# Eight small expert layers: four experts at a time as column tiles, a later k scale, and a first weight loaded early

## The chip, the cores and the metric

One core of one Trainium2 chip runs the kernel. The metric is the device time in microseconds of one execution, as a median of runs. A profile's span is about 1.8 us shorter than the time of the run it was taken from. In the profiles PE is the matrix engine and PEld its weight loads; DVE, ACT and POOL are the vector, scalar and GpSimd engines. A transfer (DMA) is issued by an engine and lands later, which is when its data may be used. The lead is the stretch before the loop is in full swing.

## The reference, cut to what matters

```python
# attention over (8 batches, 12 heads, 448 tokens, 64)
q_n, k_n = rmsnorm(q, g_q), rmsnorm(k, g_k)
attn = softmax(q_n @ k_n.T / 8) ; x = (attn @ v) as (3584, 768)
# soft mixture of experts: 8 experts with 4 slots each
logits = x @ phi                           # (3584, 32)
d = softmax over tokens ; slot_input = d.T @ x     # (32, 768)
for e in range(8):
    h = np.maximum(slot_input[e] @ w1[e], 0)       # (4, 768) @ (768, 1024)
    slot_out[e] = h @ w2[e]                        # (4, 1024) @ (1024, 768)
out = softmax over slots of logits @ slot_out      # (3584, 768)
```

The work is 24 quads of four heads each, then 16 weight matrices of 3 MB in f32 for only 32 rows, then an output of 11 MB.

## The kernel before

The loop runs over quads; one load of q brings two of them (an octet of heads). In quad Q the scores and the exponentials of Q are made, and between them the preparation of later quads: squares, row sums, `rsqrt` (Ln and Exp on ACT), scaling on POOL, transposes on PE.

```python
for Q in range(NQ + 2):
    ...                                    # score(Q, 0), square, norm, trans(Q+2, 0) ... cut
    if Q + 1 < NQ:
        trans(Q + 1, 1); evac(Q + 1, 1)    # k of the next quad: PE, then a DVE copy
    ... rowsum(Q + 4, 0)                   # DVE
    score(Q, 3) ; ... ; norm(Q - 1, 1, 1) ; rowsum(Q + 2, 1)
    score(Q, 4) ; moe_x(Q - 1)
    rsqrt(Q + 4, ...) ; scaleqk(Q + 2, 1)  # ACT, then POOL scales k with the new factors
    ...
    for i, wq in enumerate(WQ):            # WQ = [0, 2, 4, 7, 9, 11, 14, 16, 18, 19, 20, ...]
        if wq == Q: loadw(i)               # POOL issues a weight's load, f32 to bf16
```

Nine weights have room of their own. Weights 9 to 14 go where the loop's buffers were; the last goes where weight 0 was. After the loop each expert uses the weights as the stationary side:

```python
def layer1(e):                             # 48 matmuls of 4 columns, each with its 128x128 load
    hp = psum.tile([128, FC, Spe], F32, tag="sc", name="hTp")
    for fc in range(FC):
        for dc in range(DC):
            nc.tensor.matmul(hp[:, fc], wt[2 * e][:, dc, fc * 128:(fc + 1) * 128],
                             sinT[:, dc, e * Spe:(e + 1) * Spe], ...)
    nc.vector.tensor_scalar(hTs[:, e], hp, 0.0, None, op0=mybir.AluOpType.max)
# layer2(e) the same with 48 more; 8 experts, then six transposes and the output stage
```

The softmax here doesn't subtract the row's maximum and nothing guards it: scores larger than these inputs give would overflow.

Of the kernel before, what the change touches and what calls it, by code (L numbers as in the profile page):

```python
# [8 lines left out]
F32 = mybir.dt.float32  # L9
# [9 lines left out]
def kernel(  # L19
# [12 lines left out]
    nc = tc.nc  # L32
# [16 lines left out]
    NPRE = 9  # L49
    C0 = [0, 128, 256, 320]  # L50
# [22 lines left out]
    for i in range(2):  # L73
        place("rawq", 2 * 4 * NT * D, 1)
        place("rawk", 2 * 2 * NT * D, 1)
        place("free", 768, 1)
    place("rawk", 2 * 2 * NT * D, 1)
    place("sq", 2 * 2 * 2 * NT * D, 1)
    place("qkn", 2 * NT * 128, 1)
    place("vraw", 2 * 2 * NT * D, 2)  # L80
# [17 lines left out]

    def wsrc(i):
        e = i // 2  # L100
        if i % 2 == 0:
            return moe_w1[e].rearrange("(dc dp) f -> dp dc f", dp=128)
        return moe_w2[e].rearrange("(fc fp) d -> fp fc d", fp=128)
# [6 lines left out]
    wview = lambda ap, i: ap.rearrange("p (c f) -> p c f", c=DC if i % 2 == 0 else FC)  # L110
# [59 lines left out]
    gg = const.tile([128, 1], F32)  # L170
    phi_s = const.tile([128, DC, NS], BF16)
# [21 lines left out]
    def sq(t):  # L193
        return at("sq", 0).bitcast(F32).rearrange("p (t x) -> p t x", t=2)[:, t]
# [22 lines left out]
    def qkn(Q, t):  # L217
        return at("qkn", Q).rearrange("p (t s c) -> p t s c", t=2, s=NT)[:, t]
# [148 lines left out]
    vcopy(0)  # L367

    WQ = [0, 2, 4, 7, 9, 11, 14, 16, 18, 19, 20, 21, 22, NQ - 1, NQ]
    DONE = {max((b * DC + dc) // 4 * 2 + dc % 2 for dc in range(DC)): b for b in range(B)}  # L370

    for Q in range(NQ + 2):
# [3 lines left out]
        if Q == 0:  # L376
            load4(3, 1)
            loadq(2)
        elif Q + 4 < NQ:
            load4(Q + 4, 1)  # L380
# [3 lines left out]
        if Q == 0:  # L384
            rsqrt(3, 1, 2)
            scaleqk(1, 1, nc.vector)
            rowsum(2, 0)
            square(2, 1)
            rowsum(2, 1)
            trans(1, 0)  # L390
            evac(1, 0)
        else:
            if Q + 4 < NQ:
                square(Q + 4, 0)
            if Q + 2 < NQ:
                square(Q + 2, 1, True)
# [24 lines left out]
        if Q + 1 < NQ:  # L421
            trans(Q + 1, 1)
            evac(Q + 1, 1)
        if Q == 0:
            rsqrt(4, 1, 2)
            scaleqk(2, 1)
            rowsum(3, 0)
        elif Q + 4 < NQ:
            rowsum(Q + 4, 0)
# [22 lines left out]
        if on:  # L452
            score(Q, 4)
        if 0 <= Q - 1 < NQ:
            moe_x(Q - 1)
        if Q == 0:
            loadq(3)
            rowsum(4, 0)
            rsqrt(4, 0, 1)
        elif Q + 2 < NQ:  # L460
            rsqrt(Q + 4, 0 if Q + 4 < NQ else 1)
            scaleqk(Q + 2, 1)
# [9 lines left out]
        if on:  # L472
            score(Q, 6)
            ov(Q, 0, 1)
            norm(Q, 0, 0)
        if Q == 1:
# [8 lines left out]
    sinT = at("xT", 0)[:, DC * NS:2 * DC * NS].rearrange("p (dc s) -> p dc s", dc=DC)  # L485
    nc.vector.tensor_tensor(sinT, sacc[:, :DC], dinv.unsqueeze(1).to_broadcast([128, DC, NS]), op=MUL)

# [14 lines left out]

    hTs = at("xT", 1)[:, :E * FC * Spe].rearrange("p (e fc s) -> p e fc s", e=E, fc=FC)
    soTr = at("xT", 2)[:, :HD]
    so4 = at("xT", 3)[:, :HD]

    def layer1(e):
        hp = psum.tile([128, FC, Spe], F32, tag="sc", name="hTp")
        for fc in range(FC):
            for dc in range(DC):  # L510
                nc.tensor.matmul(hp[:, fc], wt[2 * e][:, dc, fc * 128:(fc + 1) * 128],  # L511
                                 sinT[:, dc, e * Spe:(e + 1) * Spe], start=(fc == 0 and dc == 0),
                                 stop=(dc == DC - 1), skip_group_check=True)
        nc.vector.tensor_scalar(hTs[:, e], hp, 0.0, None, op0=mybir.AluOpType.max)

    def layer2(e):
        sp = psum.tile([128, DC, Spe], F32, tag="misc", name="soTp")

        order = [(fc, dc) for dc in range(DC) for fc in range(FC)]
        for fc, dc in sorted(order) if e == E - 1 else order:  # L520
            nc.tensor.matmul(sp[:, dc], wt[2 * e + 1][:, fc, dc * 128:(dc + 1) * 128],  # L521
                             hTs[:, e, fc], start=(dc == 0 and fc == 0),
                             stop=(fc == FC - 1), skip_group_check=True)
        nc.vector.tensor_copy(soTr.rearrange("p (dc r s) -> p dc r s", dc=DC, r=4)[:, :, :, e * Spe:(e + 1) * Spe],
                              sp.unsqueeze(2).to_broadcast([128, DC, 4, Spe]))

    layer1(0)
    for fc in (0, FC // 2):
        nc.gpsimd.dma_start(out=wt[2 * E - 1][:, fc:fc + FC // 2], in_=wsrc(2 * E - 1)[:, fc:fc + FC // 2])
    for e in range(E):  # L530
        if e + 1 < E:
            layer1(e + 1)
        layer2(e)


    sop = psum.tile([128, HD], BF16, tag="misc", name="sop")
    for dc in range(DC):
        nc.tensor.transpose(sop[:, dc * 128:(dc + 1) * 128], soTr[:, dc * 128:(dc + 1) * 128], ident)
    nc.vector.tensor_copy(so4, sop)
# [51 lines left out]
```

## Time and profile before

| What | us |
|---|---|
| time, median | 285.3 |
| loop ends, first expert matmul | 218.2 |
| last weight has landed | 243.3 |
| output stage starts | 250.4 |
| end of the span | 282.9 |

Read the table from below: the output stage is 32.5 us of writing. It starts 7.1 us after the last weight has landed. The lines of the profile are in the prediction.

### The profile page before, as it was taken

Reading aid. Unit: us, or ns where it says so; the run is one execution under the profiler, and the core shown is the slowest. Engines: PE = TensorE matmul, PEld = TensorE weight load, DVE = VectorE, ACT = ScalarE, POOL = GpSimd, SP = SyncE. Lnnn points to the kernel's source line nnn. Section 1 sums busy time; section 2 is a strip of 40 time slices with the busy share of each in tenths; the row PEclk is TensorE's granted clock in tenths of the full one; section 3 lists DMA queues with packets and bytes.
Section 4 is the critical chain, followed back from the end, with each engine's and each line's share of the span. In section 5 each row is a group of like instructions: output and inputs, shape, how many; then the busy total and the mean of one; then the engine's idle time right before and its main releaser. Section 6 shows DMA issues by size and latency. Waiting matters only on the chain.

```text
span 282.9 us, 8520 instructions
## 1 busy us (share of the span) xinstructions
PE 222.4 (79%) x3588; PEld 148.1 (52%) x3588; DVE 179.8 (64%) x384; ACT 190.8 (67%) x276; POOL 168.4 (60%) x188
## 2 busy tenths in 40 slices
PE   7658888989898889989888998998986765788800
PEld 2325555556565556656555665665565765743300
DVE  3776677778878777787877777876564110148800
ACT  4399699888888998888889988899960000036600
POOL 0479699989688989888699896998311200000000
PEclk9955899999999999999999999999997555555555
DMA  7994999999999999999999998999999999129995
GB/s 209 325 288 132 238 255 297 243 305 231 260 259 216 279 259 260 266 267 278 284 204 238 302 220 208 233 221 230 212 211 213 211 213 210 33 92 374 420 425 248
DMA packets 42087, 69.82 MB, mean 247 GB/s; under 512 B 3776, under 2 KB 30912, under 8 KB 42048
## 3 DMA queue, kind: packets, MB, share of 16 engines
q1 hardware_dynamic: 26336, 44.05, 50.6%
q0 software_dynamic: 15392, 25.22, 49.1%
q8 instruction: 28, 0.46, 0.6%
q14 instruction: 11, 0.09, 0.1%
q10 hardware_dynamic: 320, 0.00, 0.1%
HBM read 83.46 MB, written 11.01 MB: 334 GB/s over the span
## 4 chain that ended last, share of the span: by engine, by line
PE 41%; DVE 22%; ACT 10%; issue 5%; ACTq 0%
DVE ss L210 11%; PE ov L284 10%; PE sc L272 7%; ACT arena L273 6%; PE qkTp L239 6%; PE hTp L511 4%; PE op L551 4%; PE soTp L521 4%; DVE arena L244 4%; DVE arena L294 3%; PE sinp L332 2%; PE op L552 2%; DVE arena L314 2%; ACT ss L214 1%; PE eTp L342 1%
## 5 line engine op out<-in xcount | busy, mean ns | idle before, releaser
L273 ACT ACTIVATE arena<-sc 128x896 bf16<-128x896 f32 x168 | 143.2, 921 | 7.9 <-PE sc L272 5.6
L222 POOL TENSOR_TENSOR arena<-arena,rs 128x896 bf16<-128x896 f32 x47 | 80.5, 1713 | 29.6 <-issue 11.1
L284 PE MATMUL ov<-arena 128*128 128x65 bf16 (+1 forms) x1344 | 64.4, 200 | 0.5 <-DVE arena L294 0.5
L284 PEld LDWEIGHTS <-arena 128*128 128x128 bf16 x1344 | 50.1, 99 | 20.4 <-issue 19.7
L272 PE MATMUL sc<-arena 64*128 64x448 bf16 x288 | 53.5, 368 | 7.8 <-ACT arena L273 7.1
L210 DVE TENSOR_REDUCE ss<-arena 128x14 f32<-128x896 f32 x48 | 51.6, 1076 | 5.9 <-ACT arena L202 5.9
L294 DVE TENSOR_TENSOR arena<-ov,rd 128x256 bf16<-128x256 f32 x96 | 40.7, 424 | 3.3
L555 ACT ACTIVATE wown<-op,arena 128x768 f32<-128x768 f32 x14 | 12.4, 899 | 41.2 <-PE op L552 41.2
L200 POOL TENSOR_TENSOR arena<-arena 128x896 f32<-128x896 f32 x21 | 35.4, 1686 | 0.3
L239 PE MATMUL qkTp<-ident,arena 128*128 128x128 bf16 x336 | 28.3, 227 | 6.0 <-POOL arena L222 5.4
L272 PEld LDWEIGHTS <-arena 64*128 64x128 bf16 x288 | 16.6, 93 | 25.1 <-issue 13.5
L311 PE MATMUL xTp<-ident,arena 128*128 128x128 bf16 x192 | 18.9, 222 | 12.9 <-DVE arena L294 12.9
L202 ACT ACTIVATE arena<-arena 128x896 f32<-128x896 f32 x27 | 25.6, 951 | 3.4 <-DMA arena<-in_q_dram 2.5
L239 PEld LDWEIGHTS <-arena 128*128 128x128 bf16 x336 | 20.3, 101 | 12.6 <-POOL arena L222 7.0
L293 DVE RECIPROCAL rd<-ov 128x4 f32<-128x4 f32 x96 | 17.0, 177 | 11.8 <-PE ov L284 11.4
L244 DVE COPY arena<-qkTp 128x896 bf16<-128x896 bf16 x24 | 15.0, 623 | 14.5 <-PE qkTp L239 14.5
L255 DVE TENSOR_SCALAR arena<-qkTp,gg 128x896 bf16<-128x896 bf16 (+1 forms) x26 | 17.5, 680 | 7.6 <-PE qkTp L239 7.6
L311 PEld LDWEIGHTS <-arena 128*128 128x128 bf16 x192 | 10.8, 97 | 21.6 <-DVE arena L294 17.0
L214 ACT ACTIVATE ss<-ss,eps 128x28 f32<-128x28 f32 (+1 forms) x29 | 9.1, 313 | 18.1 <-DVE ss L210 18.1
L314 DVE COPY arena<-xTp 128x1024 bf16<-128x1024 bf16 x24 | 16.4, 683 | 2.6 <-PE xTp L311 2.6
L557 DVE TENSOR_SCALAR wown<-op,arena 128x768 f32<-128x768 f32 x14 | 14.2, 1017 | 4.6 <-PE op L552 4.4
L551 PE MATMUL op<-arena,eT 32*128 32x512 bf16 x28 | 16.0, 616 | 1.4 <-ACT wown L555 0.7
(62 smaller groups left out, 215.4 us busy)
## 6 DMA issues: line engine op xcount, KB each, us to landing
wown<-in_moe_w_dram POOLq DMA_DIRECT2D x9, 1536.0 KB, 16.0
arena<-in_k_dram SPq DMA_DIRECT2D x24, 448.0 KB, 7.7
arena<-in_q_dram SPq DMA_DIRECT2D x11, 896.0 KB, 8.5
arena<-in_moe_w_dram POOLq DMA_DIRECT2D x6, 1536.0 KB, 16.8
out_dram<-wown SPq DMA_DIRECT2D x11, 768.0 KB, 8.3
arena<-in_v_dram SPq DMA_DIRECT2D x48, 128.0 KB, 6.8
arena<-in_v_dram SPq DMA_DIRECT2D x48, 96.0 KB, 6.7
out_dram<-wown SPq DMA_DIRECT2D x6, 384.0 KB, 7.0
```

The lines of the kernel that those rows point to most:

```text
L200: nc.gpsimd.tensor_tensor(s, r, r, op=MUL)
L202: nc.scalar.activation(out=s, in_=r, func=ACTF.Square)
L210: nc.vector.reduce_sum(sss[n][:, t], sq(t).rearrange("p (r d) -> p r d", d=D), axis=AX)
L222: (eng or nc.gpsimd).tensor_tensor(qkn(Q, t).rearrange("p s (r d) -> p s r d", r=2), raw(Q, t).rearrange("p r (s d) -> p s r d", d=D), rs. ...
L239: nc.tensor.transpose(pts[t][:, i], qkn(Q, t)[:, s], ident)
L244: nc.vector.tensor_copy(kT(Q).rearrange("p w (s c) -> p w s c", s=NT), pt.rearrange("p s (w c) -> p w s c", w=2))
L272: nc.tensor.matmul(sc[:, j, :S], kT(Q)[r, i // 4, c0:c0 + 128], qT(Q)[r, i // 4], start=True, stop=True)
L273: nc.scalar.activation(out=attn(i), in_=sc[:, :, :S], func=ACTF.Exp, scale=0.125)
L284: nc.tensor.matmul(ovs[half][:, c, o0:o0 + m], attn(i)[:, j, c0:c0 + 128], mov, start=(n == 0 and c == 0), stop=(n == 6), skip_group_check ...
L294: nc.vector.tensor_tensor(xq(Q).rearrange("p c (h w d) -> p c h w d", h=2, w=2)[:, 2 * half:2 * half + 2, :, w], o[:, :, :, :D], rd.to_bro ...
L311: nc.tensor.transpose(xps[Q][:, i], xq(Q)[:, i % 4, i // 4 * 128:i // 4 * 128 + 128], ident)
L551: nc.tensor.matmul(op[:, 0], eTtok(j, s), so4[r, :512], start=True, stop=True, tile_position=tp)
```

## The change

Its intent has three parts. **Experts**: the weights become the moving side, 512 columns long; the 32 slots of the input are the stationary side, and four experts sit side by side in the four 32-column strips of the array. Each strip computes all 32 slots for its expert, a mask (`own`) keeps the four that are its own, and a 0/1 matrix (`sel`) adds the strips up at the end. **Loop**: k is scaled at the start of the next quad, from factors that exist by then, and its transpose and copy stand behind the row sums. The load of a later k moves behind that scaling, and the loop's buffers are regrouped (lines cut here). **Early weights**: weight 0 is issued in the lead, weights 1 to 8 one quad earlier.

```diff
+    WORD = [(l, EG * g + j) for g in range(E // EG) for l in range(2) for j in range(EG)]
...                                                     (experts)
+        if Q == 2:
+            for j in range(EG):
+                r = slice(NS * j, NS * j + NS)
+                nc.vector.tensor_copy(sel[r]..., ident[r, r]...to_broadcast([NS, EG, NS]))
+                for g in range(E // EG):
+                    nc.vector.reduce_sum(own[r, g:g + 1], ident[r, o:o + Spe], axis=AX)
...
+    def layer1(g):
+        hp = psum.tile([128, 2, 512], F32, tag="sc", name="hp")
+        for dc in range(DC):
+            for i in range(2):
+                for j in range(EG):
+                    nc.tensor.matmul(hp[NS * j:NS * j + NS, i], sinT[:, dc],
+                                     wt[2 * EG * g + j][:, dc, i * 512:i * 512 + 512], ...,
+                                     tile_position=(0, NS * j))
...
+    layer2(0, range(EG))
+    layer2(1, (0, 1))
+    layer2(1, (2,))
+    layer2(1, (3,), range(FC // 2))
+    layer2(1, (3,), range(FC // 2, FC))
...                                                     (loop)
-            scaleqk(Q + 2, 1)                           # end of quad Q
+            if Q + 1 < NQ:
+                scaleqk(Q + 1, 1)                       # start of quad Q
+        if Q and Q + 1 < NQ:                            # now behind score(Q, 4)
+            trans(Q + 1, 1)
+            evac(Q + 1, 1)
...                                                     (early weights)
-    WQ = [0, 2, 4, 7, 9, 11, 14, 16, 18, 19, 20, 21, 22, NQ - 1, NQ]
+    loadw(0)
+    WQ = [-1, 1, 3, 6, 8, 10, 13, 15, 17, 19, 20, 21, 22, NQ - 1, NQ]
```

More of the change, by code (lines that the diff above doesn't have):

```diff
@@ L49 @@
     NPRE = 9
+    EG = 4
     C0 = [0, 128, 256, 320]
@@ L71, in place @@
             sizes.append(elems)
-    for i in range(2):
-        place("rawq", 2 * 4 * NT * D, 1)
-        place("rawk", 2 * 2 * NT * D, 1)
-        place("free", 768, 1)
+    place("rawq", 2 * 4 * NT * D, 1)
+    place("sq0", 2 * 2 * NT * D, 1)
+    place("free", 768, 1)
+    place("rawq", 2 * 4 * NT * D, 1)
     place("rawk", 2 * 2 * NT * D, 1)
-    place("sq", 2 * 2 * 2 * NT * D, 1)
-    place("qkn", 2 * NT * 128, 1)
-    place("vraw", 2 * 2 * NT * D, 2)
+    place("free", 768, 1)
+    place("rawk", 2 * 2 * NT * D, 1)
+    place("sq1", 2 * 2 * NT * D, 1)
+    place("qkn0", NT * 128, 1)
+    place("vraw", 2 * 2 * NT * D, 1)
+    place("rawk", 2 * 2 * NT * D, 1)
+    place("qkn1", NT * 128, 1)
+    place("vraw", 2 * 2 * NT * D, 1)
     place("kT", 2 * S, 1)
@@ L96, in at @@
         return arena[:, off:off + elems]
+    WORD = [(l, EG * g + j) for g in range(E // EG) for l in range(2) for j in range(EG)]
     def wsrc(i):
-        e = i // 2
-        if i % 2 == 0:
+        l, e = WORD[i]
+        if l == 0:
             return moe_w1[e].rearrange("(dc dp) f -> dp dc f", dp=128)
@@ L109 @@
     wplace += [arena[:, o:o + WSZ], wplace[0]]
-    wview = lambda ap, i: ap.rearrange("p (c f) -> p c f", c=DC if i % 2 == 0 else FC)
+    wview = lambda ap, i: ap.rearrange("p (c f) -> p c f", c=(DC, FC)[WORD[i][0]])
     wt = [wview(wplace[i], i) for i in range(2 * E)]
@@ L170 @@
     gg = const.tile([128, 1], F32)
+    sel = const.tile([128, 128], BF16)
+    own = const.tile([128, E // EG], F32)
     phi_s = const.tile([128, DC, NS], BF16)
@@ L193, in sq @@
     def sq(t):
-        return at("sq", 0).bitcast(F32).rearrange("p (t x) -> p t x", t=2)[:, t]
+        return at(f"sq{t}", 0).bitcast(F32)
     def square(Q, t, pool=False):
@@ L217, in qkn @@
     def qkn(Q, t):
-        return at("qkn", Q).rearrange("p (t s c) -> p t s c", t=2, s=NT)[:, t]
+        return at(f"qkn{t}", 0).rearrange("p (s c) -> p s c", s=NT)
     def scaleqk(Q, t, eng=None):
@@ L378 @@
             loadq(2)
-        elif Q + 4 < NQ:
-            load4(Q + 4, 1)
         if on:
@@ L394 @@
                 square(Q + 4, 0)
+            if Q + 1 < NQ:
+                scaleqk(Q + 1, 1)
+            if Q + 4 < NQ:
+                load4(Q + 4, 1)
             if Q + 2 < NQ:
@@ L420 @@
             norm(Q - 1, 1, 0)
-        if Q + 1 < NQ:
-            trans(Q + 1, 1)
-            evac(Q + 1, 1)
         if Q == 0:
-            rsqrt(4, 1, 2)
-            scaleqk(2, 1)
+            trans(1, 1)
+            evac(1, 1)
             rowsum(3, 0)
@@ L458 @@
             rowsum(4, 0)
-            rsqrt(4, 0, 1)
+            rsqrt(4)
         elif Q + 2 < NQ:
             rsqrt(Q + 4, 0 if Q + 4 < NQ else 1)
-            scaleqk(Q + 2, 1)
         if on:
@@ L475 @@
             norm(Q, 0, 0)
+        if Q == 2:
+            for j in range(EG):
+                r = slice(NS * j, NS * j + NS)
+                nc.vector.tensor_copy(sel[r].rearrange("p (r s) -> p r s", r=EG),
+                                      ident[r, r].unsqueeze(1).to_broadcast([NS, EG, NS]))
+                for g in range(E // EG):
+                    o = NS * j + (EG * g + j) * Spe
+                    nc.vector.reduce_sum(own[r, g:g + 1], ident[r, o:o + Spe], axis=AX)
         if Q == 1:
@@ L484, with turn, layer2 @@
     nc.vector.reciprocal(dinv, sacc[:, DC])
-    sinT = at("xT", 0)[:, DC * NS:2 * DC * NS].rearrange("p (dc s) -> p dc s", dc=DC)
+    sinT = at("xT", 0)[:, :DC * NS].rearrange("p (dc s) -> p dc s", dc=DC)
     nc.vector.tensor_tensor(sinT, sacc[:, :DC], dinv.unsqueeze(1).to_broadcast([128, DC, NS]), op=MUL)
+    hTs = {}
+    def layer1(g):
[3 more added lines that the diff above has]
+                for j in range(EG):
+                    nc.tensor.matmul(hp[NS * j:NS * j + NS, i], sinT[:, dc], wt[2 * EG * g + j][:, dc, i * 512:i * 512 + 512],
+                                     start=(dc == 0), stop=(dc == DC - 1), skip_group_check=True, tile_position=(0, NS * j))
+        h = at("x", 2 * g)
+        for i in range(2):
+            nc.vector.tensor_scalar(h[:, i * 512:i * 512 + 512], hp[:, i], 0.0, own[:, g:g + 1], op0=mybir.AluOpType.max, op1=MUL)
+        return h
+    def turn(g, h):
+        ht = psum.tile([128, FC, 128], BF16, tag="misc", name="ht")
+        for fc in range(FC):
+            nc.tensor.transpose(ht[:, fc], h[:, fc * 128:fc * 128 + 128], ident)
+        hTs[g] = at("x", 2 * g + 1).rearrange("p (fc c) -> p fc c", fc=FC)
+        nc.vector.tensor_copy(hTs[g], ht)
+    def layer2(g, js, fcs=range(FC)):
+        for fc in fcs:
+            for c0, c1 in ((0, 512), (512, HD)):
+                for j in js:
+                    nc.tensor.matmul(sop[NS * j:NS * j + NS, c0 // 512, :c1 - c0], hTs[g][:, fc, NS * j:NS * j + NS],
+                                     wt[2 * EG * g + EG + j][:, fc, c0:c1], start=(g == 0 and fc == 0),
+                                     stop=(g == 1 and fc == FC - 1), skip_group_check=True, tile_position=(0, NS * j))
+    h = layer1(0)
+    for fc in (0, FC // 2):
+        nc.gpsimd.dma_start(out=wt[2 * E - 1][:, fc:fc + FC // 2], in_=wsrc(2 * E - 1)[:, fc:fc + FC // 2])
+    turn(0, h)
+    h = layer1(1)
     def eTtok(j, s):
@@ L501 @@
         nc.vector.reciprocal(cinv[:, j:j + 2], cs[:, :, :SO])
-    hTs = at("xT", 1)[:, :E * FC * Spe].rearrange("p (e fc s) -> p e fc s", e=E, fc=FC)
-    soTr = at("xT", 2)[:, :HD]
-    so4 = at("xT", 3)[:, :HD]
-    def layer1(e):
-        hp = psum.tile([128, FC, Spe], F32, tag="sc", name="hTp")
-        for fc in range(FC):
-            for dc in range(DC):
-                nc.tensor.matmul(hp[:, fc], wt[2 * e][:, dc, fc * 128:(fc + 1) * 128],
-                                 sinT[:, dc, e * Spe:(e + 1) * Spe], start=(fc == 0 and dc == 0),
-                                 stop=(dc == DC - 1), skip_group_check=True)
-        nc.vector.tensor_scalar(hTs[:, e], hp, 0.0, None, op0=mybir.AluOpType.max)
@@ L516, in layer2 @@
-    def layer2(e):
-        sp = psum.tile([128, DC, Spe], F32, tag="misc", name="soTp")
-        order = [(fc, dc) for dc in range(DC) for fc in range(FC)]
-        for fc, dc in sorted(order) if e == E - 1 else order:
-            nc.tensor.matmul(sp[:, dc], wt[2 * e + 1][:, fc, dc * 128:(dc + 1) * 128],
-                             hTs[:, e, fc], start=(dc == 0 and fc == 0),
-                             stop=(fc == FC - 1), skip_group_check=True)
-        nc.vector.tensor_copy(soTr.rearrange("p (dc r s) -> p dc r s", dc=DC, r=4)[:, :, :, e * Spe:(e + 1) * Spe],
-                              sp.unsqueeze(2).to_broadcast([128, DC, 4, Spe]))
@@ L527 @@
-    layer1(0)
-    for fc in (0, FC // 2):
-        nc.gpsimd.dma_start(out=wt[2 * E - 1][:, fc:fc + FC // 2], in_=wsrc(2 * E - 1)[:, fc:fc + FC // 2])
-    for e in range(E):
-        if e + 1 < E:
-            layer1(e + 1)
-        layer2(e)
-    sop = psum.tile([128, HD], BF16, tag="misc", name="sop")
-    for dc in range(DC):
-        nc.tensor.transpose(sop[:, dc * 128:(dc + 1) * 128], soTr[:, dc * 128:(dc + 1) * 128], ident)
-    nc.vector.tensor_copy(so4, sop)
+    turn(1, h)
+    sop = psum.tile([128, 2, 512], F32, tag="sc", name="sop")
@@ new lines @@
+    layer2(0, range(EG))
[3 more added lines that the diff above has]
+    layer2(1, (3,), range(FC // 2, FC))
+    so = at("xT", 2)[:, :HD]
+    so4 = at("xT", 3)[:, :HD]
+    parts = ((0, 512, nc.scalar.copy), (512, HD, nc.vector.tensor_copy))
+    for c0, c1, copy in parts:
+        copy(so[:, c0:c1], sop[:, c0 // 512, :c1 - c0])
+    for c0, c1, copy in parts:
+        sp = psum.tile([128, 512], F32, tag="misc", name="sp")
+        nc.tensor.matmul(sp[:, :c1 - c0], sel, so[:, c0:c1], start=True, stop=True)
+        copy(so4[:, c0:c1], sp[:, :c1 - c0])
```

## The prediction

> **What bounds the kernel now.** I read the page first, then the stretches (busy time of each engine by stage), the chain of waits, the timeline of one quad, and the landings of the weight transfers.
>
> The page's slices, and then the same split where the behaviour changes:
>
> ```profile
> PEclk9955899999999999999999999999997555555555
> DMA  7994999999999999999999998999999999129995
> ...
> q1 hardware_dynamic: 26336, 44.05, 50.6%
> q0 software_dynamic: 15392, 25.22, 49.1%
> ```
>
> ```profile
> 20.00:30.00 10.00, 7.52 (x70) 4.64 (x68) 6.56 (x13) 9.30 (x16) 9.40 (x10) 0.50 0.65 148
> 30.00:135.00 105.00, 90.65 (x1432) 60.58 (x1430) 82.63 (x181) 91.20 (x133) 90.12 (x97) 0.99 1.10 263
> 135.00:145.00 10.00, 8.48 (x135) 5.83 (x135) 7.62 (x18) 9.05 (x14) 7.66 (x9) 1.00 0.93 247
> ...
> 170.00:180.00 10.00, 8.46 (x134) 5.50 (x134) 8.34 (x18) 8.70 (x13) 7.68 (x9) 1.00 0.89 223
> 180.00:217.00 37.00, 32.91 (x586) 22.42 (x584) 23.67 (x63) 27.22 (x38) 20.76 (x27) 0.98 1.13 217
> 217.00:243.00 26.00, 16.00 (x574) 15.77 (x575) 3.57 (x16) 0.00 (x0) 1.50 (x2) 0.50 1.08 198
> 243.00:250.00 7.00, 6.38 (x214) 6.13 (x211) 1.38 (x6) 0.00 (x0) 0.00 (x0) 0.50 0.02 5
> 250.00:283.00 33.00, 16.95 (x56) 7.01 (x55) 14.49 (x15) 12.38 (x14) 0.00 (x0) 0.50 0.81 334
> ```
>
> Columns: length, busy us of PE, PEld, DVE, ACT, POOL, then granted clock, DMA share, GB/s. The reader is to see four stages: lead (to 30 us), quad loop (to 217), experts (217 to 250), output (to 283). The DMA share is 1.06 to 1.13 nearly everywhere from 5 to 243 us; packets of two queues overlap, so about 1.1 is what full engines look like here. From 243 to 250 it is 0.02: every weight has landed, and PE alone still works. In the output it is DMA again (11 MB at 420 GB/s is 26 of the 33 us).
>
> The loop looks bound by a chain through engines:
>
> ```profile
> 119.96 0.40 PE qkTp L239 x7
> 120.36 0.02 issue
> 120.38 0.62 DVE arena L244
> 121.01 0.99 DVE ss L210
> 122.00 0.10 DVE rd L293
> 122.10 0.02 issue
> 122.12 0.42 DVE arena L294
> 122.55 1.00 DVE ss L210
> 123.55 0.02 issue
> 123.58 0.33 ACT ss L214
> ```
>
> The transpose of the next k, its eviction on DVE, two row sums behind it, and ACT's Ln, which waits for the second sum. The list of waits for 27 to 217 us gives its price:
>
> ```profile
> ACT ss L214 <- DVE ss L210: 12.5, 19, 1.0
> ```
>
> A quad takes 7.75 us, or 8.88 where the slot weights are worked on (starts of ACT's Square, 118.55 and 126.51 or 109.87).
>
> The experts are neither matmul work nor weight transfers:
>
> ```profile
> 227.79 2.37 issue
> 230.16 0.33 PE hTp L511 x7
> 230.48 1.28 PE soTp L521 x48
> 231.76 1.28 PE hTp L511 x48
> 233.04 0.67 PE soTp L521 x25
> 233.71 2.37 issue
> ```
>
> 7+48+48+25 is 128 matmuls, with their loads 256 instructions, then PE stands 2.4 us. The four gaps (1.82, 2.37, 2.37, 2.60) are 5.9 to 6.1 us apart from end to end, and the trace has an instruction transfer of 16384 bytes beside each: 256 instructions of 64 bytes. I read this as PE running dry of instructions.
>
> Landings of the last weights, from the trace: 196.9, 204.9, 212.9, 220.9, 228.4, 235.9, and the last one's halves at 239.6 and 243.3: one per 7.5 us.
>
> **What the Trainium skill says.** "DMA: Bandwidth & Descriptors", section Queues, rings and completion order: each DMA engine goes round the queues it has work for. So a weight in flight takes from q, k and v. The trace agrees: in 70 to 75 us the weight queue moved 160 GB/s and the other 65, and in 75 to 80, the weight landed, 26 and 309. The same page, section Where 436 GB/s comes from, gives 435 GB/s for the fabric. Weights alone write 209 GB/s of bf16 and so read 418 of f32: the engines are at their rate, and only idle time can be won.
> "TensorE: Matmul & The Clock Gate", section Part 3: Packing small matmuls, measures 2.38 times for three column tiles of 512 columns. The kernel before has no pure column tiles of that length; its 64x64 pairs (four of 448 columns in 0.57 us) do overlap. The same page, section Back-to-back issue gap, gives N/1.2 ns cold and about N/2.4 warm; 24 four-column matmuls tell nothing of that here, but the 512-column ones of the output start 0.43 us before the next, which is 512/1.2 at the granted 0.50.
>
> **The change, part by part.**
>
> 1. Experts. 768 matmuls of 4 columns with 768 loads of 128x128 go, and 8 DVE steps each of ReLU and copy. In come, for each group of four experts, 48 matmuls of 512 columns in rounds of four: 12 x 512 = 6144 columns, and in layer 2 64 matmuls, 8 x 768 = 6144 columns if four run side by side. Cold that is 5.1 us each, warm 2.6. The second layer 2 is split for the arriving weights: experts 0 and 1 together, then 2, then 3 in halves, so 3 x 6144 columns, 15.4 cold or 7.7 warm. In all 6 x 6144: 31 us cold, 15.4 warm, plus about 4 for ReLU, turning and the row sums cs. 532 pairs fewer are 1064 instructions fewer; the 242 left span two refills, and a refill's 128 matmuls now last longer than the 5.9 us that it takes. So the four gaps (9.2 us) go.
> But the last weight still lands last, in the slot of the first, and after it come half of expert 3 (3072 columns, 1.3 to 2.6 us), two copies (about 0.55, from 0.81 for 896 columns of ACT), the select matmul (0.4 to 0.6) and two copies again: 3.3 to 5 us, where the kernel before needs 250.4 - 243.3 = 7.1. That is 2 to 3.8 us won, if PE has caught up.
>
> 2. The k scale moves from the end of a quad, behind this quad's Ln and Exp, to the start of the next, and the k transpose and its eviction move behind the row sums. The chain above is cut: the eviction's 0.62 and its wait of 0.63 leave DVE's way to the second sum, POOL stops waiting for factors, and ACT's 12.5 us of waits should nearly vanish. ACT then has 7.75 - 0.63 = 7.1 us a quad. In slot quads PE's extra 2 us (logits 0.7, sums and turn 1.3) keep a wait. By engines alone the loop could lose 10 to 11 us. POOL needs 6.8 us a quad and 0.9 per weight issue every second: just enough.
>
> 3. The first weight is issued behind the first v copy, where POOL pauses 18.4 to 19.96, instead of at 27.16, and weights 0 to 8 one quad earlier. It fills the hole of 20 to 30 us.
>
> **Why part 2 is not worth its 10 us.** The DMA has 24 quads of q, k and v and 16 weights of 7.5 us. The quads' part: queue q1's 50.6% of 282.9 us is 143, less 26 for the output is 117, over the 1.05 that this queue shows when it alone fills the engines is 111, or 4.6 us a quad. A stretch of seven quads with three weights needs 7 x 4.6 + 3 x 7.5 = 55 us, and takes 7 x 8.11 = 56.8 now. At 7.4 us a quad it would be 51.8: the transfers would not keep up. So the sum to use is DMA idle before 243.3. Counted from packets in flight (engines below sixteen): 2.2 in 0 to 5, 4.0 in 20 to 30, 1.1 in 135 to 145, 1.7 in 170 to 180, 0.4 elsewhere, 9.4 in all, of which the first 2.2 stay. Part 3 fills nearly 4, the faster loop most of 3. The last weight then lands 5.5 to 7 us sooner, at about 237. The loop ends near 210.5, and the first layers run 210.5 to about 230 partly cold, so expert 3 waits for its weight.
> Output starts at 237 + 4.2 = 241.2 instead of 250.4: 9.2 us. The output keeps its 32.5 us. 285.2 - 9.2 = 276.0; I allow half a microsecond for unfilled holes and say 276.4.
>
> **Rivals.**
> A. Column tiles do not run side by side (one set of rows, no fast loads). Then the experts need 4 x 10.2 = 41 us warm, output starts near 255 and the time is 286 to 290. Against it the skill's 2.38; for it, that no row here shows it. About 6%.
> B. PE stays cold. The output's 32-row matmuls are 80% busy at clock 0.5 and never warm it, and expert 2 and 3 alone use a quarter of the columns. All cold, PE ends near 245.5 and output starts near 248: 282 to 283. Against: full-width rounds of layer 1 run 5 us without a gap. About 15%.
> C. The loop is not held by DMA and gives its whole 10 us. Then the weights pile up behind, the last lands as computed, and the end hardly moves; at best all idle is filled: 236 + 3.3, so about 274.
> D. Early weights starve q, k, v (the queues alternate) and the first quads stall. The landings leave 2 us of slack for the second q octet (21.2 against a Square at 23.4); the engines stay full, so this moves the loop rather than the last landing. Up to 1 us.
>
> **Range and chances.** Floor 273 to 274 (C), centre 276.4, B at 282, A above. Eight times in ten 273 to 281. Two per cent faster is 279.5: chance 0.77; within 0.21, mostly B; slower 0.02.
>
> **What would show it.** Right: no Ln waits of 0.6 to 1.0; DMA share near 1.1 through 20 to 30 and the loop; the last landing at 236 to 239; PE waiting for a transfer ahead of expert 3; output start 4 us after. Wrong: quads at 7.1 with DMA share below 1 (DMA was not the bound), tiles starting 0.2 us or more apart within a round (A), clock 0.5 through the experts with PE working past the landing (B).

## The result, and the profile after

The changed kernel takes 274.15 us in the median (273.31 to 277.19, four runs), the kernel before 285.34 in the same comparison. The ratio is 0.9631, with a 95% interval of 0.9555 to 0.9706. Ratios here and below are the mean time of one kernel's runs over that of the other's of the same rounds, so not quite the ratio of the medians.

| What | before | after | gain |
|---|---|---|---|
| loop ends | 218.2 | 212.8 | 5.4 |
| last weight has landed | 243.3 | 237.0 | 6.3 |
| output stage starts | 250.4 | 240.2 | 10.2 |
| output stage | 32.5 | 32.3 | 0.2 |

First the page's clock and DMA rows of the changed kernel, then three stretches (columns as in the prediction):

```profile
PEclk9955797799999999999999997999999599975555
DMA  6999999999999999999999999999999999639995
```

```profile
20.00:30.00 10.00, 7.49 (x70) 4.55 (x68) 6.54 (x13) 8.89 (x14) 8.69 (x9) 0.50 1.05 223
...
207.00:233.00 26.00, 20.27 (x316) 11.17 (x317) 7.64 (x17) 0.28 (x1) 2.37 (x3) 0.87 1.16 211
233.00:240.00 7.00, 3.57 (x18) 1.72 (x18) 0.51 (x2) 1.02 (x2) 0.00 (x0) 1.00 0.36 64
```

The hole of the DMA between 20 and 30 us is filled (share 1.05 where it was 0.65). In the experts' stage the clock is mostly 1.00, where it was 0.50.

The waits of the changed kernel for 27 to 212 us hold this line in place of the 12.5 us:

```profile
ACT ss L226 <- DVE ss L222: 0.4, 1, 0.4
```

So the loop part does what it was meant to: the chain through k's copy and the row sums is gone. A quiet quad takes 7.0 us (starts of ACT's Square at 95 and 102) instead of 7.75.

The column tiles, in the timeline of PE's first layer:

```profile
220.01 0.39 PE L516 MATMUL hp<-wown,arena 128*32 128x512 bf16 x1
220.01 0.40 PE L516 MATMUL hp<-arena 128*32 128x512 bf16 x3
220.23 0.38 PE L516 MATMUL hp<-wown,arena 128*32 128x512 bf16 x1
220.24 0.39 PE L516 MATMUL hp<-arena 128*32 128x512 bf16 x3
```

Four matmuls of 512 columns start together and the next four 0.22 us later: four for the price of one (one matmul of 512 columns every 0.43 us at clock 0.5 in the output before would be 0.215 at 1.0, an estimate). The tail in the timeline, from the landing of the last weight's first half:

```profile
233.30 1.46 PE L534 MATMUL sop<-wown,arena 128*32 128x512 bf16 x8 [0.76 <-DMA wown<-in_moe_w_dram]
...
237.02 1.46 PE L534 MATMUL sop<-wown,arena 128*32 128x512 bf16 x8 [2.25 <-DMA wown<-in_moe_w_dram]
...
238.51 0.59 ACT L571 CAST arena<-sop 128x512 bf16<-128x512 f32 x1 [28.60 <-PE sop L534]
...
239.15 0.73 PE L574 MATMUL sp<-arena,sel 128*128 128x512 bf16 x2 [0.67 <-ACT arena L571]
...
239.56 0.59 ACT L575 CAST arena<-sp 128x512 bf16<-128x512 f32 x1 [0.46 <-PE sp L574]
...
240.20 0.37 PE L587 MATMUL op<-arena,eT 32*128 32x512 bf16 x1 [0.32 <-ACT arena L575]
```

PE waits for each half, and the output starts 3.2 us after the last landing. So, in the profiled runs, 3.9 us of the gain are the shorter tail (7.1 - 3.2) and 6.3 are the earlier landing. The number is close to the prediction's 276.4, but that says nothing yet about why the landing moved. One thing stands in the trace of the changed kernel that the prediction never named, on DVE at the end of quad 2:

```profile
45.36 0.36 DVE L493 COPY sel<-ident 32x128 bf16<-32x128 bf16 x1
...
45.86 1.50 DVE L493 COPY sel<-ident 32x128 bf16<-32x128 bf16 x1
...
47.50 1.53 DVE L493 COPY sel<-ident 32x128 bf16<-32x128 bf16 x1
```

and POOL beside it:

```profile
45.64 1.68 POOL L212 TENSOR_TENSOR arena<-arena 128x896 f32<-128x896 f32 x1
47.27 1.71 POOL L234 TENSOR_TENSOR arena<-arena,rs 128x896 bf16<-128x896 f32 x1
```

Columns: start, duration, engine, line, operation. These are the copies that build `sel`. The second ends at 47.36 and POOL's square at 47.32, the third at 49.03 and POOL's scaling at 48.98: each copy ends when POOL's instruction does. The block stands in DVE's queue from 45.36 to about 49.5, some 4.2 us, and then PE shows a wait of 2.61 us (at 50.23) and ACT one of 2.44 (at 51.79). The Trainium skill, "SBUF — State Buffer", section SBUF: two separate sides, says that VectorE, in some of its modes, and GpSimd share one pair of ports under an exclusive lock held for a whole instruction, and that the other blocks. The trace fits that: two of the copies end within 0.05 us of an instruction of POOL that lasts 1.7 us. Which mode these copies run in is not shown.

A second wait in the loop belongs to the data. ACT's timeline of the changed kernel:

```profile
38.78 0.95 ACT L214 ACTIVATE arena<-arena 128x896 f32<-128x896 f32 x1 [2.52 <-DMA arena<-in_q_dram]
```

ACT waited 2.52 us for a q that came late; it lands at 38.8, and in the kernel before, where ACT asks for it at 37.83, at 37.8. Rival D of the prediction puts such a wait down to the early weights. The record says otherwise: f_experts_loop, with the new loop and the weights at their old places, has the same wait,

```profile
39.15 0.95 ACT L214 ACTIVATE arena<-arena 128x896 f32<-128x896 f32 x1 [2.51 <-DMA arena<-in_q_dram]
```

and so has k_lead_late (2.17 us at 39.03), while f_early, with the early weights and the old loop, has none there. So the wait goes with the loop part: this loop asks for q sooner than q comes.

### The profile page after: what moved, and what is told of

Its sections match the earlier page's. It is cut to its first block, busy times and chain, and to the rows that moved or that the text cites. A ratio compares the mean times of both kernels' runs of the same rounds, so it can differ in the third digit from the quotient of the medians.

```text
span 272.5 us, 7454 instructions
## 1 busy us (share of the span) xinstructions
PE 218.0 (80%) x3056; PEld 137.7 (51%) x3056; DVE 185.0 (68%) x387; ACT 190.8 (70%) x276; POOL 168.3 (62%) x188
## 4 chain that ended last, share of the span: by engine, by line
ACT 36%; PE 22%; DMA 18%; DVE 7%; issue 7%; POOL 4%; SPq 0%; POOLq 0%; ACTq 0%; DVEq 0%
ACT arena L285 28%; DMA arena<-in_q_dram 11%; DMA wown<-in_moe_w_dram 7%; ACT arena L214 5%; PE op L587 4%; PE sc L284 3%; PE ov L296 3%; POOL arena L234 3%; DVE ss L222 2%; PE qkTp L251 2%; PE sc L280 2%; PE sinp L344 2%; PE xTp L323 2%; PE op L588 2%; PE lg L333 2%
## 5 line engine op out<-in xcount | busy, mean ns | idle before, releaser
L296 PEld LDWEIGHTS <-arena 128*128 128x128 bf16 x1344 | 50.3, 99 | 23.8 <-issue 23.1
L284 PE MATMUL sc<-arena 64*128 64x448 bf16 x288 | 54.5, 377 | 5.3 <-ACT arena L285 4.1
L251 PE MATMUL qkTp<-ident,arena 128*128 128x128 bf16 x336 | 29.4, 232 | 6.3 <-POOL arena L234 5.8
L251 PEld LDWEIGHTS <-arena 128*128 128x128 bf16 x336 | 20.5, 103 | 17.9 <-POOL arena L234 8.6
L284 PEld LDWEIGHTS <-arena 64*128 64x128 bf16 x288 | 15.4, 93 | 23.7 <-issue 12.4
L280 PE MATMUL sc<-arena 64*64 64x448 bf16 x96 | 14.7, 383 | 12.3 <-ACT arena L285 12.3
L571 ACT CAST arena<-sop 128x512 bf16<-128x512 f32 x1 | 0.6, 586 | 28.6 <-PE sop L534 28.6
L241 POOL CAST arena<-arena 128x384 bf16<-128x384 f32 x24 | 12.0, 501 | 8.3 <-DMA arena<-in_v_dram 4.5
L323 PE MATMUL xTp<-ident,arena 128*128 128x128 bf16 x192 | 16.2, 231 | 0.5 <-DVE arena L306 0.5
L587 PE MATMUL op<-arena,eT 32*128 32x512 bf16 x28 | 14.9, 571 | 0.7 <-ACT wown L591 0.3
```

What stands on the lines that cost most here:

```text
L251: nc.tensor.transpose(pts[t][:, i], qkn(Q, t)[:, s], ident)
L280: nc.tensor.matmul(sc[r, j, :S], kT(Q)[r, j, 384:], qT(Q)[r, j], start=True, stop=True, tile_position=(64 * hh, 64 * hh))
L284: nc.tensor.matmul(sc[:, j, :S], kT(Q)[r, i // 4, c0:c0 + 128], qT(Q)[r, i // 4], start=True, stop=True)
L296: nc.tensor.matmul(ovs[half][:, c, o0:o0 + m], attn(i)[:, j, c0:c0 + 128], mov, start=(n == 0 and c == 0), stop=(n == 6), skip_group_check ...
L323: nc.tensor.transpose(xps[Q][:, i], xq(Q)[:, i % 4, i // 4 * 128:i // 4 * 128 + 128], ident)
L587: nc.tensor.matmul(op[:, 0], eTtok(j, s), so4[r, :512], start=True, stop=True, tile_position=tp)
```

## The experiments

Twelve kernels ran, in three groups of four; each group ran on one chip and shared its runs of the kernel before (medians 285.26, 284.34 and 284.59). Two theories stood against each other:

- **Transfers (the prediction's).** The DMA engines are full. The last landing moves by the idle time that is filled and by nothing else; a faster loop only waits for its data.
- **Pace.** A weight behind the first nine is issued only when its quad is done with the buffer. The last weights go where the loop's own buffers were, so the landing follows the loop, wherever the loop's time comes from.

All in one table first, so that the runs can be compared. "w9" is weight 9, the first that needs a buffer of the loop; "idle" is the DMA idle up to the last landing, counted as in the prediction from engines below sixteen (in each row some 1.5 us of it belong to the last microseconds themselves). The last five columns come from the profiled run, the median and the ratio from all runs. The profiled run is the slowest of its kernel in f_experts_loop, k_experts_lead, k_wq and k_fewer_tail and the fastest in k_lead, so two or three us between the landings of two rows can be the runs' own.

| Kernel | us | ratio, 95% | w9 issued | last landing | landing less w9 | idle | output starts |
|---|---|---|---|---|---|---|---|
| before | 285.3 | 1 | 182.9 | 243.3 | 60.4 | 10.9 | 250.4 |
| after | 274.15 | 0.9631 (0.9555 to 0.9706) | 177.0 | 237.0 | 60.0 | 8.8 | 240.2 |
| f_experts | 286.98 | 1.0069 (1.0028 to 1.0111) | 188.6 | 248.4 | 59.8 | 20.5 | 252.3 |
| f_loop | 280.12 | 0.9816 (0.9780 to 0.9852) | 173.1 | 238.0 | 64.9 | 8.6 | 245.4 |
| f_early | 285.53 | 1.0016 (0.9982 to 1.0051) | 183.9 | 243.8 | 59.9 | 7.2 | 251.3 |
| f_experts_loop | 275.98 | 0.9645 (0.9579 to 0.9711) | 178.0 | 239.8 | 61.8 | 10.3 | 243.0 |
| k_lead | 272.07 | 0.9578 (0.9538 to 0.9618) | 173.6 | 233.5 | 59.9 | 8.0 | 236.7 |
| k_fewer | 273.82 | 0.9628 (0.9595 to 0.9662) | 175.2 | 235.5 | 60.3 | 21.9 | 239.3 |
| k_experts_lead | 279.98 | 0.9842 (0.9808 to 0.9877) | 183.0 | 242.7 | 59.7 | 14.2 | 247.1 |
| k_wide | 284.93 | 1.0041 (0.9998 to 1.0083) | 182.3 | 242.6 | 60.3 | 8.7 | 250.6 |
| k_lead_late | 274.46 | 0.9632 (0.9586 to 0.9679) | 174.3 | 237.2 | 62.9 | 8.0 | 240.4 |
| k_wq | 272.06 | 0.9553 (0.9514 to 0.9592) | 176.2 | 235.7 | 59.5 | 7.6 | 239.2 |
| k_best | 270.40 | 0.9492 (0.9452 to 0.9531) | 172.6 | 232.3 | 59.7 | 6.0 | 234.9 |
| k_fewer_tail | 269.45 | 0.9455 (0.9407 to 0.9504) | 177.1 | 233.8 | 56.7 | 12.0 | 237.1 |

Before the single runs, read two columns. "Landing less w9" is 59.5 to 60.4 us in ten of the fourteen rows, while the issue itself moves over 16 us. And the idle column has no order with the times: 7.2 us stands at 285.5 us, 21.9 at 273.8.

What holds that issue? By the program POOL issues weight 9 at the end of quad 19. In the kernel before, POOL's own scaling of a k is the last to read the buffer; it ends at 182.59, and the issue follows at 182.89. In the changed kernel the last reader is a row sum on DVE that ends at 174.05, but POOL, which has the copies of a v in front, issues at 177.02. So there the place in POOL's order holds weight 9 by 3 us more than the buffer. No run moves this issue alone.

### Each part alone

**f_experts**: the kernel before with the experts' part only.

```diff
-    weights in the order of experts, layer1(e), layer2(e)   # as before
+    WORD, sel, own at Q == 2, layer1(g), layer2(g, ...)     # as in the change
```

> Experts as column tiles alone, loop and weight schedule of before. The loop gets no faster, so the last weight lands at about 243 us as before. Theory (the experts' part is worth the tail after the last landing): output starts 3.2 to 3.5 us after the landing instead of 7.1, so about 281.5 us, 3.5 to 4 less than before. Rival (the four instruction gaps of 9.2 us were the loss): 9 us less, 276. The constants built on DVE inside quad 2 cost up to 4 us there, which could eat the gain; then 284 or so.

Slower by 0.7%, so all three of the times expected were missed. The mechanism of the tail is there (output 3.9 us after the landing instead of 7.1), yet the loop ends at 223.4 instead of 218.2. DVE in its quad 2:

```profile
45.48 4.07 DVE L486 COPY sel<-ident 32x128 bf16<-32x128 bf16 x1
```

A copy of 32x128 elements that takes 4.07 us, until 49.55; POOL works beside it from 45.24 to 49.49 on a weight's issue, a square and a scaling. PE and ACT then show waits of 4.71 (at 51.07) and 5.46 us (at 53.78). The loop ends 5.2 us later and the landing comes 5.1 later; the shorter tail takes 3.2 of that back, and the output starts 1.9 us later than before. So the small block costs about 5 us here, more than the tail gains.

**f_loop**: the loop's part only.

```diff
-            scaleqk(Q + 2, 1)                 # end of quad Q
+                scaleqk(Q + 1, 1)             # start of quad Q
-            trans(Q + 1, 1); evac(Q + 1, 1)
+            trans(Q + 1, 1); evac(Q + 1, 1)   # behind score(Q, 4); buffers regrouped, one k load later
```

> Loop reordering alone, experts and weight schedule of before. Theory (transfers hold the whole): the loop shortens by 3 to 5 us, Ln waits vanish, the experts still take 33 us on PE behind the loop, so 280 to 282 us. Rival (loop free of the DMA): 10 us less, 275.

The ratio 0.9816 has an interval from 0.9780 to 0.9852, so whether it passes 2% is unclear. The time, 280.1, is the one that the transfers' theory gave; PE's old experts follow either way, so the landing has to decide. The loop ends 5.1 us sooner (213.1). The landing moves 5.3 us, with an idle time that fell by 2.3 us only. By the prediction's sum of idle time that can't be.

**f_early**: the early weights only.

```diff
+    loadw(0)
-    WQ = [0, 2, 4, 7, 9, 11, 14, 16, 18, 19, ...]
+    WQ = [-1, 1, 3, 6, 8, 10, 13, 15, 17, 19, ...]
```

> Earlier weights alone. Theory of the prediction (idle DMA filled, 4 us): last landing near 239.5, but PE's experts still follow the loop by 33 us, so the time is 284 to 285.5, the same. Rival (earlier weights starve q, k and v in the first quads): the loop ends later, 286 to 288.

This is the cleanest test of the transfers' theory: idle falls from 10.9 to 7.2 us, and nothing is won: the landing, which was to come near 239.5, is at 243.8 against 243.3 (time 1.0016, as both theories allow). Filling the hole in the lead only brings early weights early; weight 9 still waits for quad 19.

**f_experts_loop**: everything but the early weights.

```diff
-    loadw(0)                                  # from the changed kernel
-    WQ = [-1, 1, 3, 6, 8, 10, 13, 15, 17, 19, ...]
+    WQ = [0, 2, 4, 7, 9, 11, 14, 16, 18, 19, ...]
```

> The change without the earlier weights. Theory of the prediction (DMA idle time counts): the hole of 20 to 30 us is back, last landing 3.5 to 4 us later than the full change's 237.0, so 278 us. Rival (the last landing follows the quad that frees the slots, plus eight weights): no starving in quads 2 and 3, so as fast as the full change or up to 2 us faster, 272 to 274.

0.9645, against 0.9631 of the whole change: the early weights are worth nothing that these runs can tell. The time, 276.0, lies between the two that were expected. The logarithms of the three single parts sum to -1.0%, the whole has -3.8%: the parts help each other, for f_loop alone still ends with the old tail (7.4 us after the landing), and the stall at `sel`, 5 us in f_experts, costs about half of that beside the new loop.

### Where the stall and the landing come from

**k_lead**: the changed kernel, with `sel` and `own` built in the lead.

```diff
+    for j in range(EG): ... sel, own ...      # in the lead, 2.6 to 3.8 us
-        if Q == 2:
-            for j in range(EG): ... sel, own ...
```

> The full change with the two constants (sel, own) built on DVE in the idle lead (2.7 to 5.1 us) instead of at the end of quad 2. Theory now (the last landing follows the loop: quad 19 frees the arena, then seven weights): the stall of 2.4 us on ACT and 2.6 on PE at 50 us goes, the loop and the last landing come 2 to 4 us earlier, 270 to 272 us. Rival (the prediction's: transfers fill the time anyway): only the 0.5 us of idle DMA at 50 to 55 is won, 273.5 to 274.5.

DVE's timeline in the lead:

```profile
2.60 0.12 DVE L201 COPY sel<-ident 32x128 bf16<-32x128 bf16 x1
```

0.12 us (0.18 and 0.19 for the other three) for a copy that takes up to 1.53 in the changed kernel and 4.07 in f_experts; POOL's first long instruction starts at 7.48. The loop ends 3.5 us sooner than in the changed kernel (209.3), w9 is issued 3.5 us sooner, the last weight lands 3.5 us sooner: one to one. By ratios the move is worth 0.5% (0.9631 to 0.9578), by medians 2.1 us; the intervals overlap, and the profiled run of k_lead is its fastest. The wait at 50 us is gone; ACT waits 2.60 us for a q at 53.60 instead.

**k_experts_lead**: f_experts with the same move.

```diff
+    for j in range(EG): ... sel, own ...      # f_experts, with the block in the lead
-        if Q == 2:
-            for j in range(EG): ... sel, own ...
```

> Experts alone with the constants built in the lead. Theory (the 1.7 us that experts alone lost are the stall in quad 2): loop end and last landing back at 218 and 243.5, output starts 3.3 us after the landing, 281 to 282 us. Rival (column tiles themselves cost the loop or the landing something): still 285 to 287.

From 1.0069 to 0.9842. With the block out of the way the loop ends at 218.0, as before, the landing is that of before, and the experts give what their tail gives: the output starts 4.5 us after the landing, 3.3 sooner than before. Here the granted clock was 0.5 from 242.5 to 245.9, and the tail is 1.3 us longer than the changed kernel's. This settles that the block, and not the column tiles, made f_experts slow. It also answers the rival of f_experts: the instruction gaps, 9.2 us of idle PE, were not worth 9 us, for the last weight bounds this stage.

**k_fewer**: the changed kernel without the loads of weights 1 and 2 (wrong: three experts' weights share one buffer).

```diff
+    wplace[1] = wplace[2] = wplace[3]
-            if wq == Q:
+            if wq == Q and i not in (1, 2):
```

> The full change without the loads of weights 1 and 2 (experts 1 and 2 read expert 3's first layer; the result is wrong on purpose). 15 us of transfers less, at 34 to 67 us. Prediction's account (transfer time adds up to the last landing): the landing comes 8 us or more earlier, 266 or less. Theory now (loop, then the weights behind quad 19): only q, k, v waits of the first quads go, 2.5 to 4 us, 270.5 to 272, with some 10 us more of idle DMA.

Two transfers of 7.5 us go, out of the loop's early quads. Windows 35 to 75 us, first the changed kernel, then this one (columns as in the prediction):

```profile
35.00:75.00 40.00, 32.36 (x477) 21.61 (x476) 32.56 (x74) 32.65 (x47) 32.84 (x34) 0.91 1.07 253
```

```profile
35.00:75.00 40.00, 32.39 (x495) 21.96 (x491) 33.41 (x77) 33.87 (x49) 32.55 (x36) 0.96 0.68 185
```

The DMA share falls from 1.07 to 0.68, and the engines do hardly more in the same 40 us. The seven quads that start at 57.0 in the changed kernel and end at 108.9 take 51.8 us here too (starts of ACT's Square at 56.3 and 108.1). The landing moves 1.5 us, the median 0.3; the 266 or less of the prediction's account is far off, and the 2.5 to 4 us of the other theory did not come either (ACT still waited 1.59 us for q at 38.60). Were the loop bound by transfers here, 15 us fewer of them would have shown. The high share is what the loop's data and the weights cost when there is time for them; it is not what holds the loop.

**k_fewer_tail**: the same with weight 10, which is loaded after w9 (also wrong).

```diff
+    wplace[10] = wplace[8]
-            if wq == Q:
+            if wq == Q and i != 10:
```

> The full change without the load of weight 10, one of those behind quad 19 (expert 6 reads expert 4's first layer; wrong on purpose). 7.5 us of transfers less in the tail. Theory (60 us of transfers from quad 19 to the last landing): the landing comes 7.5 us earlier, near 229.5, and PE, which ends expert 2 near 232.5, becomes the bound: output starts near 237, 3 us less, 271. If the tail were as free as the early transfers, whose removal gave 0.3 us: 274.

One transfer less behind w9, and the ratio is 0.9455 instead of 0.9631, about 5 us (3.3 between the two profiled runs). One weight in the tail is worth more than two in the loop. It did not land where I had expected it, 229.5, but at 233.8: weight 11 is now next, and it is issued only at 190.3, at the end of quad 21, so the DMA had 1.9 us of idle in 190 to 195. So here the issue takes part of what the shorter transfers give.

### The experts' waits, and the early weights

**k_wide**: the kernel before with 48 moving columns instead of 4 in each first-layer matmul (wrong; the ReLU reads the first four of each).

```diff
-        hp = psum.tile([128, FC, Spe], ...)
+        hp = psum.tile([128, FC, 48], ...)
-                                 sinT[:, dc, e * Spe:(e + 1) * Spe]
+                                 sinT.rearrange("p dc s -> p (dc s)")[:, dc * 22 + e * Spe:dc * 22 + e * Spe + 48]
```

> The kernel before, with 48 moving columns instead of 4 in each first-layer matmul of the experts (result wrong on purpose). At clock 0.5, 48 columns are 40 ns against the 27 ns a pair takes now: 384 x 13 ns = 5 us more of PE work. Theory (PE waits for 256 instructions every 5.9 us): the work fits into the gaps, which shrink, output starts at 250 to 251, time 285 to 286. Rival (the gaps are something else, matmul time adds): 289 to 290.

```profile
223.47 1.35 PE L511 MATMUL hTp<-arena,wown 128*128 128x48 bf16 x39 [0.69 <-issue]
229.39 0.44 PE L511 MATMUL hTp<-arena,wown 128*128 128x48 bf16 x7 [1.65 <-issue]
```

Twelve times the columns cost nothing that these runs resolve: output at 250.6 against 250.4. The waits at the same places shrink from 1.82 and 2.37 us to 0.69 and 1.65, and the starts behind them keep their distance of 5.9 us. PE's work fills a wait whose period something else sets. That fits the reading of the prediction, which no run shows directly: 256 instructions in a transfer of 16384 bytes each 5.9 us. The page's list of queues supports it: the kernel before has the row "q8 instruction: 28, 0.46, 0.6%" (packets, MB, share), and the changed kernel

```profile
q8 instruction: 24, 0.39, 0.6%
```

Four packets fewer, where the prediction counted 1064 instructions fewer, 4.2 times 256.

**k_lead_late**: k_lead with the weight schedule of before.

```diff
-    loadw(0)
-    WQ = [-1, 1, 3, 6, 8, 10, 13, 15, 17, 19, ...]
+    WQ = [0, 2, 4, 7, 9, 11, 14, 16, 18, 19, ...]
```

> Constants in the lead, but the weight schedule of before (first weight at quad 0, the others as before). Theory (the loop's pace decides, transfers only by delaying q, k and v): within 1 us of the version with early weights, 271.5 to 273. The prediction's account (filling the hole of 20 to 30 us is worth nearly 4 us): 275.5 to 276.5.

0.9632 against k_lead's 0.9578: beside the fast loop the early schedule is worth 1.5 us by the ratios, and the difference of the two intervals allows up to 3.3. The time, 274.5, meets neither expectation, of 271.5 to 273 nor of 275.5 to 276.5. The trace shows another reason than the filled hole: w9 is issued at 174.3, nearly as in k_lead, but weight 8 is still in flight until 181.6, 7.2 us later, and the landing comes 62.9 us after w9 instead of 59.9. The three kernels with the late schedule and the new loop are the ones above 60.4 in the table: overlaps of weight 8 and w9 of 5.3 (f_experts_loop), 7.2 and 7.7 us (f_loop) go with 61.8, 62.9 and 64.9. Kernels with 4.3 to 4.9 us of overlap still have 60. This is a pattern of three runs, not a test of its own.

**k_wq**: k_lead with weights 1 and 2 one quad later.

```diff
-    WQ = [-1, 1, 3, 6, 8, 10, 13, ...]
+    WQ = [-1, 2, 4, 6, 8, 10, 13, ...]
```

> Constants in the lead, early first weight, but weights 1 and 2 one quad later (quads 2 and 4). Theory: the wait for q of 2.6 us at 53 us shrinks as no weight takes from q, k, v at 34 to 42; 270 to 272 against 272.1. If the lost time at 44 to 62 is not the weights': 272 and more.

0.9553 against 0.9578, overlapping: not resolved. Its profiled run, its slowest (273.65 us), still had a wait of 3.49 us for q at 39.2, so the schedule doesn't cure that wait in every run.

**k_best**: k_wq with the last weight in quarters, so that less work is left behind the last landing.

```diff
-    for fc in (0, FC // 2):                   # last weight: two transfers
+    for fc in range(0, FC, 2):                # four transfers
-    layer2(1, (3,), range(FC // 2)); layer2(1, (3,), range(FC // 2, FC))
+    for fc in range(0, FC, 2): layer2(1, (3,), range(fc, fc + 2))
```

> As the one before, and the last weight in quarters instead of halves, so that 4 matmuls and not 8 are left after the last landing. 0.6 us less between last landing and start of output: 2.6 instead of 3.2; the time 0.5 us under the one before, which the rounds hardly resolve.

Correct, and the fastest kernel that is: 270.4 us, 0.9492. By the ratios that is 1.7 us under k_wq, but the intervals overlap. The output starts 2.6 us behind the landing instead of 3.2. Its window 35 to 75 us:

```profile
35.00:75.00 40.00, 35.39 (x567) 24.28 (x567) 34.17 (x75) 38.02 (x55) 38.32 (x41) 1.00 1.11 278
```

No long stall is left there: ACT is busy 38.0 of the 40 us and POOL 38.3, and the same DMA engines move 278 GB/s where they moved 253. The loop ends at 208.4, 9.8 us before that of before; in k_wq's slow profiled run the same loop, with its wait for q, ended at 213.2. The last weight lands at 232.3. That is 3.7 us below the 236 that the prediction gave as the landing with all idle time filled.

## Why the prediction was right or wrong

The time was right, 276.4 against 274.15 and inside the range, but in part by luck: errors stood against each other in it.

**The tail: right in kind, mis-sized.** Column tiles run four side by side, and the instruction waits vanish. Rival A falls (rounds 0.22 us apart) and rival B falls (clock 1.0 from 218.1 to 242.0 us). The term "237 + 4.2" took the middle of 3.3 to 5 us; it measured 3.2, just below its low end, with the clock at 1.0; k_experts_lead, at 0.5 in its tail, measured 4.5. One microsecond was left there.

**The landing: right number, wrong step.** The step that failed is "the transfers would not keep up. So the sum to use is DMA idle before 243.3". Seven quads with three weights were said to take 55 us, and 51.8 to be out of reach; the changed kernel took 51.85 for seven (starts of ACT's Square at 57.02 and 108.87), and k_fewer, without weight 2 in that stretch, the same. The 4.6 us a quad rested on packets' durations as if they were fixed. They are not: the mean of queue q1's 1024-byte packets was 65 ns in the kernel before and 60 in the changed one, that of 1792 bytes 100 and 94. So a share of 1.1 was no proof of full engines. What took its place is the pace: w9 is issued at the end of quad 19, and 60 us later the last weight lands (12.9 us for weight 9, then 8.8 and 8.4, then four times 7.5). In that tail the transfers do bind, as k_fewer_tail shows. Idle time fell by 2.1 us only, and the landing moved 6.3.

**The loop's 10 us: right, then argued away.** "By engines alone the loop could lose 10 to 11 us" holds: k_best shows 9.8. The changed kernel shows 5.4 of them. The block at quad 2 took 2.4 to 2.6 us (k_lead removes it), and by its trace q's late landing 2.52; so a transfer binds at single places, but not throughout, for quiet quads run at 7.0 us. Rival C came nearest in its cause, "the loop is not held by DMA", but was wrong in "the end hardly moves": k_lead's loop ended 3.5 us sooner and so did its landing.

**Early weights: wrong.** "Part 3 fills nearly 4" is true of the hole, but the early weights are worth between nothing and 1.5 us instead of 4 (f_early, f_experts_loop, k_lead_late; the intervals of the last two allow up to 3.3). Rival D had a wait for q of the right kind and the wrong cause: it comes with the new loop and late weights too.

**Not seen at all: the block that builds `sel`.** The part-by-part working names no DVE time for it; it held DVE for 4.2 us in the changed kernel and cost about 2 us in the median there (k_lead) and 5 us of the loop in f_experts. So the prediction credited nearly 4 us to the filled hole and most of 3 to the idle in the loop, and the 6.3 us came from the loop's pace: up to 9.8 us to be had, less those lost to the late q and to this block. The signs that it named as right all came but one: no Ln waits, a full hole, PE waiting for the last weights, a landing between 236 and 239; the output started 3.2 us after it, not 4. None of them tells the two theories apart. The sign named as wrong does, quads at 7.1 us with a DMA share below 1, and it took k_fewer to make it: quiet quads of 7.0 us (starts at 94.1, 101.1, 108.1) and 0.68 between 35 and 75 us.

**Misread on the way.** The starts that the prediction names give 7.96 us for a quad and 8.68 for one with slot weights, not 7.75 and 8.88; 7.75 is right for other quads, and the mean of 8.11 that it used holds. And "the engines are at their rate" sets 418 GB/s read against a page's 435 for the ports of SBUF, where these transfers wrote 209; what the traces show is the 7.5 us of a weight.

**Left open.** Why the packets of q, k and v last shorter in some kernels; whether the buffer or the place in POOL's order should be moved to issue w9 sooner; the exact worth of the early weights; and why the changed kernel's runs spread over 273.3 to 277.2 us. The late q is a candidate (in the profiled runs it holds ACT at 38.8 in the changed kernel, at 53.6 in k_lead, and in k_best only at 142.7, for 0.76 us), but no run tests it.

## What to carry to other kernels

Ask what holds back the issue of the next transfer, its buffer or its place in the issuing engine's order, before asking how full the DMA engines are: in ten of fourteen kernels here the last landing followed the issue of one weight by 60 us, whatever the idle time. Price also the one-off constants, and build them where nothing else needs the engine, for a copy of 0.12 us became one of up to 4 us inside a busy loop. When the rows are few, let the weights move and set the strips of the array side by side; and to learn whether a transfer binds, take it away in an experiment, as its busy share alone misled here.

## What the Trainium skill lacked or had wrong

- "TensorE: Matmul & The Clock Gate", section Part 3: Packing small matmuls, has three column tiles of 512 columns at 2.38 times. Four are not measured there. Here four, each in a strip of 32, cost what one costs: rounds of four start 0.22 us apart at clock 1.0.
- "Runtime: NRT & Kernel Launch", section Instruction fetch mechanics, has the blocks of 16 KiB, 256 instructions, but calls the crossing of one mostly hidden and gives no time for a wait. Here 256 matmuls and loads went with one transfer of 16384 bytes on the queue of kind "instruction" each 5.9 us, and in the kernel before PE stood idle for 9.2 us beside four of them; k_wide shows that the period is not set by the matmuls' work.
- "DMA: Bandwidth & Descriptors", section Queues, rings and completion order, says that an engine goes round its queues packet by packet, but not with what shares of the time, nor that the duration of equal packets in a trace differs between kernels (65 and 60 ns in the mean for 1024 bytes). A share of 1.07 fell to 0.68 in k_fewer without a faster loop.
- "SBUF — State Buffer", section SBUF: two separate sides, has a lock that fits what is seen, but doesn't say that a copy which waits can lose to POOL's next instruction too: a copy of 0.12 us alone took 1.50 and 1.53 us behind one instruction of POOL, and 4.07 in f_experts, where three followed each other.
